# Another order of all work in a gated convolution block with a feed-forward: which queue issues ten of the loads, and when

## The chip, the core and the metric

The kernel runs on one NeuronCore of a Trainium2 chip. The metric is device time in microseconds (us), the median of three runs of the same kernel. The program's own profile gives, for one execution, when each instruction ran on each engine: PE (matrix products), DVE (elementwise), ACT (elementwise and eviction of results from PE's accumulators), POOL (GpSimd: here small statistics and DMA issues) and SP (here DMA issues alone).

## What is computed

With x = A_q of 2048 rows and 640 columns, the reference is, in short:

```python
k_shift = sum over t<4 of k[s - 3 + t] * shift_k[:, 3 - t]       # short causal convolution
kv = k_shift * v
y  = causal convolution of kv with ssm_k along 2048 rows (by FFT) + kv * ssm_D
h  = x + layernorm(x) * y
h2 = h + (silu(layernorm(h) @ w_gate) * (layernorm(h) @ w_up)) @ w_down    # F = 1728
```

All inputs and the output are bf16.

## The kernel before

The 2048 rows are four blocks of 512 (j = 0 to 3). For each block the kernel loads ssm_k (`load_g`), k (`load_k`), v and x, makes the spectrum G of ssm_k and the spectrum X of kv by matmuls with a fixed basis WF (`transform`, `forward`; line 329, evicted by ACT at line 319), multiplies and adds spectra of this block and of earlier ones on DVE (`window`, `mac`; lines 537 to 600), goes back with the basis WI (`inverse`, line 698), makes h and its row statistics, normalizes and transposes it (`turn_h`), and feeds it through the feed-forward layer (`ffn`): gate and up products (line 769), SiLU and product (lines 783 to 787), down product (lines 833 and 845). The feed-forward of block j stands among the convolution work of block j+1.

ssm_k must be transposed. Block 0's is transposed by PE (`transposed`, line 411). Blocks 1 to 3 are first regrouped by one ACT copy (`g_turned`, line 419) and then turned by four DMA transposes on SP (line 404); k of blocks 1 to 3 is turned by four DMA transposes each, straight from DRAM. kv is made by PE (the taps, line 490) and a DVE product with v (line 513). Nine matmuls of line 882 between two parts of block 0's taps feed nothing. ACT's sums for the row statistics of x and h are at lines 606 and 629; GpSimd finishes the statistics (lines 610 to 636).

All work is recorded as 923 operations with a number each; a recorded operation has a list of the buffers that it reads and writes. The tuple `ORDER` then says in which order they are handed out, and with that the order on each engine and queue, since every engine works through its own in turn. A negative number ~n hands out operation n in its other form: an eviction of ACT goes to DVE or back, a load goes to GpSimd's queue in place of SP's, and a sum of two buffers on DVE becomes an adding DMA from GpSimd:

```python
def load(nbytes, fn, w, r=()):
    return plan.add("sp", nbytes, lambda: fn(nc.sync), r, w, ("pq", nbytes, lambda: fn(nc.gpsimd)))
def added(ns, fn, to, what, reads, write, n=1):
    plan.add("dve", ns, fn, reads, [write], ("add", ..., lambda: nc.gpsimd.dma_start(out=to(), in_=what(), accum_op=ALU.add, ...)))
```

The order also decides the memory: large buffers lie in an arena of 22 units, and a buffer takes a unit when its first operation is handed out, so a load can have to wait until the last reader of the unit's buffer before is done. An accumulator `ps` has four places, a `row` five.

Of the kernel before, what the change touches and what calls it, by code (L numbers as in the profile page):

```python
# [47 lines left out]
    0, 1, 2, 3, 16, 18, -20, 5, 4, 8, 17, 186, 9, 20, 22, 7, 10, 11, -22, 24, -26, 23, 26, 75, 76, 13, 15, 12, 6,  # L48
    77, 78, 79, 193, 80, 81, 82, 34, 35, 14, 38, -40, 36, -38, 92, 32, 27, 93, 96, 97, 40, -42, 88, 89, 30, 94,
    95, 98, 99, 101, 102, 90, 91, 28, 84, 85, 42, 43, 44, 121, 119, 103, 29, 104, 118, 47, 48, 86, 87, 100, 45,  # L50
    46, 120, 105, 106, 49, 50, 124, 55, 51, 56, 83, 31, 52, 107, 108, 57, 58, 113, 33, 114, 53, 54, 123, 109, 110,
    67, 68, 125, 115, 126, 116, 111, 112, 194, 198, 192, 199, 117, 69, 70, 195, 59, 60, 71, 72, 196, 200, 201, 63,
    64, 61, 62, 73, 74, 127, 212, 65, 130, 66, 128, 202, 213, 207, 129, 134, 208, 131, 187, 203, 189, 197, 214,
    215, 216, 190, 209, 210, 204, 133, 205, 270, 188, 221, 224, 225, 223, 175, 132, 138, 122, 211, 206, 217, 143,
    144, 137, 136, 141, 222, 142, 140, 146, 218, 145, 147, 148, 226, 228, 227, 191, 229, 265, 178, 153, 154, 149,
    150, -165, -162, 135, 139, 151, 152, 235, 236, 245, 246, 237, 238, 162, 163, 220, 157, 219, 252, 247, 165,
    166, 248, 249, 231, 232, 409, 240, 155, 241, 156, 158, 159, 320, 325, 177, 336, 335, 180, 332, 173, 233, 253,
    242, 234, 239, 243, 244, 321, 174, 324, 328, 331, 271, 160, 250, 167, 310, 255, 334, 314, 338, 339, 168, 169,
    251, 337, 170, 176, 312, 333, 340, 341, 185, 416, 259, 323, 327, 171, 261, 172, 256, 326, 322, 329, 330, 269,
    -309, -255, 418, 267, 179, 309, 260, 311, 316, 347, 313, 315, 268, 317, 342, 262, 318, 230, 319, 353, 346,  # L60
    343, 350, 358, 357, 417, 266, 421, 422, 354, 381, 380, 385, 263, 257, 384, 383, 382, 345, 419, 349, 423, 348,
    386, 355, 424, -259, 264, 272, 273, 413, 344, 351, 352, 184, 361, 420, 360, 430, 431, 274, 275, 356, 359, 362,
    363, 375, 415, 432, 433, 435, 436, 376, 425, 437, 377, 438, 367, 370, 426, 277, 283, 378, 276, 279, 278, 290,
    427, 428, 410, 182, 181, 291, 282, 288, 289, 366, 434, 371, 414, 183, 281, 286, 287, 280, 284, 285, 295, 293,
    412, 296, 479, 294, 292, 439, 379, 297, 365, 369, 368, 411, 364, 372, 539, 483, 373, 374, 496, 503, 298, 299,
    429, 440, 387, 399, 300, 301, 389, 390, 391, 400, 401, 304, 392, 393, 402, 441, 442, 444, 448, 445, 305, 447,
    306, 307, 388, 302, 303, 394, 395, 396, 397, 404, 443, 475, 476, 477, 449, 451, 450, 446, 452, 498, 405, 406,
    478, 484, -482, 407, 408, 587, 588, 591, 454, 592, 455, 458, 459, 562, 485, -487, 590, 589, 593, 480, 456,
    457, 561, 565, 482, -617, 563, 398, 460, 461, 468, 469, 462, 463, 464, 564, 575, 566, 567, 470, 471, 465, 466,
    467, 472, 473, 453, 619, 576, 583, 502, 582, 584, -586, 586, 474, 490, 491, 579, 499, 541, 540, 544, 542, 620,  # L70
    543, 545, 546, 492, 493, 623, 624, 626, 618, 627, 569, 487, 577, 578, 549, 547, 580, 494, 581, 501, 489, 625,
    548, 551, 500, 497, 504, 403, 550, 552, 553, 488, 495, 505, 506, 507, 508, 509, 555, 568, 572, 554, 556, 558,
    557, 559, 560, 632, 633, 628, 640, 641, 636, 637, 634, 635, 642, 643, 638, 571, 513, 629, 630, 639, 519, 520,
    631, 510, 514, 521, 522, 570, 573, 574, 644, 526, 622, -646, 595, 611, 617, 511, 515, 516, 512, 517, 518, 687,
    525, 601, 612, 524, 527, 523, 528, 710, 682, 529, 530, 535, -534, 534, 531, 537, 532, 594, 596, 713, 646, 538,
    681, 602, 603, 606, 607, 707, 677, 685, 678, 680, 604, 608, 613, 614, 708, 597, 688, 609, 647, 649, 648, 651,
    598, 536, 806, 599, 805, 808, 650, 766, 765, 807, 809, 810, 811, 693, 709, 652, 654, 653, -622, 655, 695,
    -680, 768, 767, 711, 769, 770, 771, 683, 706, 800, 801, 802, -804, 690, 684, 665, 666, -687, -697, 712, 714,
    660, 758, -695, 661, 667, 668, 669, 759, 762, 662, 663, 670, 671, 689, 804, 761, 760, 656, 763, 691, -693,
    672, 673, 782, 657, 780, 764, 658, 674, 659, 664, 675, 676, 700, 702, 701, 787, 779, 788, 786, 790, 789, 791,  # L80
    792, 697, 783, 781, 784, 795, 773, 615, 785, 772, 775, 774, 776, 698, 777, 778, 699, -704, 704, 794, 793, 797,
    796, 798, 799, 812, 814, 815, 816, 705, 715, 716, 717, 718, 719, 600, 720, 605, 610, 817, 813, -758, 818, 819,
# [908 lines left out]
```

## Time and profile before

| | before |
|---|---|
| runs | 250.96, 251.34, 253.92 us; median 251.34 |
| the profiled execution | a span of 251.4 us from first to last instruction; the profile gives no other time of it |
| clock granted to PE | 1.000 |
| busy | PE 237.3 us, DVE 197.7, ACT 173.9, POOL 54.0 |
| DMA | 33.66 MB, 134 GB/s on the mean; SP's queue 21.38 MB, GpSimd's 11.96 MB |
| chain that ended last | PE 56%, ACT 17%, DMA 10%, DVE 9% |

"Idle before" in such a profile is time in which an engine had nothing running ahead of an instruction, and what ended it. "us to landing" of a DMA counts from its issue until the last byte is in. A window row gives the length, then busy time and instructions of PE, PE's weight loads, DVE, ACT and POOL, the clock, the share of the DMA engines' time that was busy, and GB/s.

### The profile page before, as it was taken

The page shows a single profiled execution, that of the slowest core. Times are in us where ns is not written, and L with a number is a line of the kernel's source. Part 1 is how long each engine was busy: PE and PEld are TensorE (multiplying, and loading weights), DVE is VectorE, ACT ScalarE, POOL GpSimd, SP SyncE. Part 2 cuts the span into 40 slices and gives each one's busy share as a digit, 9 for nine tenths or more (in the row PEclk, how much of TensorE's full clock was granted, in tenths as well). Part 3 has the DMA queues.
Part 4 walks back from the last instruction along what each step waited for, and adds up shares of the span by engine and source line. Part 5 has one row for each costly group of instructions (what it writes and reads, how often), then busy time and mean ns, then how long its engine had stood idle before and what let it go on. Part 6 is the DMA issues. An engine that isn't in the chain of part 4 may idle for free.

```text
span 251.4 us, 5138 instructions
## 1 busy us (share of the span) xinstructions
PE 237.3 (94%) x2113; PEld 153.0 (61%) x2125; DVE 197.7 (79%) x249; ACT 173.9 (69%) x300; POOL 54.0 (21%) x54
## 2 busy tenths in 40 slices
PE   3869997999999999999999999999999999999994
PEld 3447675788777677444465676454456785465662
DVE  2379999999999999999999989999999542131222
ACT  2449998999999976975988789983542865325100
POOL 0002003231540313220270404263612110000030
PEclk9999999999999999999999999999999999999999
DMA  5995699774998654685345468889592200000052
GB/s 156 376 212 163 127 324 352 231 197 92 165 246 292 202 81 81 105 154 133 79 66 146 86 99 194 148 146 163 98 224 29 26 0 3 0 0 3 0 78 78
DMA packets 37283, 33.66 MB, mean 134 GB/s; under 512 B 22470, under 2 KB 32076, under 8 KB 37260
## 3 DMA queue, kind: packets, MB, share of 16 engines
q1 hardware_dynamic: 31884, 21.38, 32.1%
q0 software_dynamic: 5376, 11.96, 25.9%
q8 instruction: 16, 0.26, 0.4%
q14 instruction: 7, 0.06, 0.1%
HBM read 16.29 MB, written 4.59 MB: 83 GB/s over the span
## 4 chain that ended last, share of the span: by engine, by line
PE 56%; ACT 17%; DMA 10%; DVE 9%; issue 4%; SPq 3%; DVEq 0%; ACTq 0%; POOLq 0%
PE ps L769 24%; PE ps L845 22%; ACT arena L319 7%; DMA arena<-in_A_ssm_k_dram 7%; PE ps L698 5%; DMA arena<-arena 3%; ACT sg L785 2%; PE ps L490 2%; SPq L404 2%; ACT junk L606 1%; PE ps L329 1%; PE ps L833 1%; DVE arena L674 1%; DVE arena L663 1%; DVE arena L662 1%
## 5 line engine op out<-in xcount | busy, mean ns | idle before, releaser
L769 PE MATMUL ps<-arena,wgu 128*128 128x512 bf16 (+1 forms) x668 | 116.7, 328 | 1.4 <-ACT sg L809 0.5
L769 PEld LDWEIGHTS <-wgu 128*128 128x128 bf16 x680 | 66.2, 98 | 45.3 <-issue 1.4
L845 PE MATMUL ps<-wd,tT 128*128 128x320 bf16 x416 | 59.1, 299 | 0.0
L845 PEld LDWEIGHTS <-tT 128*128 128x128 bf16 x416 | 39.8, 98 | 17.2 <-issue 1.8
L542 DVE TENSOR_TENSOR arena<-arena 128x2560 bf16<-128x2560 bf16 x30 | 44.1, 1484 | 0.2
L783 ACT ACTIVATE sg<-ps 128x1024 bf16<-128x1024 f32 (+1 forms) x28 | 26.9, 968 | 20.3 <-PE ps L769 19.7
L329 PE MATMUL ps<-arena,WF 128*128 128x320 bf16 x176 | 29.8, 299 | 1.2 <-ACT arena L319 0.9
L785 ACT CAST sg<-ps 128x1024 bf16<-128x1024 f32 (+1 forms) x23 | 23.0, 998 | 6.9 <-PE ps L769 3.1
L319 ACT CAST arena<-ps 128x320 bf16<-128x320 f32 (+1 forms) x48 | 25.2, 583 | 1.9 <-DVE arena L545 1.1
L610 POOL TENSOR_TENSOR sm<-sm,neghalf 128x4 f32<-128x4 f32 (+1 forms) x10 | 16.6, 1659 | 43.4 <-DVE sm L646 43.1
L787 DVE TENSOR_TENSOR tT<-sg,sg 128x1024 bf16<-128x1024 bf16 (+1 forms) x23 | 15.5, 673 | 11.5 <-ACT sg L785 11.5
L243 POOL DMA_DIRECT2D arena<-arena x11 | 13.3, 1211 | 47.4 <-DVE arena L542 11.2
L329 PEld LDWEIGHTS <-WF 128*128 128x128 bf16 x176 | 17.1, 98 | 10.0 <-issue 2.3
L606 ACT ACTIVATE junk<-arena 128x640 bf16<-128x640 bf16 x28 | 20.8, 744 | 1.3 <-DVE arena L709 1.3
L545 DVE TENSOR_TENSOR arena<-arena 128x2560 bf16<-128x2560 bf16 x14 | 20.7, 1487 | 0.2
L319 ACT ACTIVATE arena<-ps 128x640 bf16<-128x640 f32 (+1 forms) x32 | 20.2, 655 | 0.3
L698 PE MATMUL ps<-arena,WI 128*128 128x320 bf16 x96 | 15.7, 299 | 0.9 <-issue 0.6
L850 ACT ACTIVATE row<-ps,sm 128x640 bf16<-128x640 f32 x12 | 9.5, 791 | 8.2 <-PE ps L845 8.0
L709 DVE SCALAR_TENSOR_TENSOR arena<-arena,sm,ps 128x640 bf16<-128x640 bf16 x16 | 13.6, 876 | 1.8 <-ACT ps L707 1.8
L852 POOL DMA_DIRECT2D out_dram<-row x12 | 11.7, 1153 | 14.1 <-ACT row L850 14.1
L707 ACT ACTIVATE ps<-ps,sm 128x640 f32<-128x640 f32 x16 | 12.1, 770 | 3.7 <-PE ps L698 3.5
L698 PEld LDWEIGHTS <-WI 128*128 128x128 bf16 x96 | 9.0, 97 | 5.6 <-issue 1.3
(91 smaller groups left out, 240.8 us busy)
## 6 DMA issues: line engine op xcount, KB each, us to landing
arena<-arena POOLq DMA_DIRECT2D x11, 640.0 KB, 6.1
arena<-in_A_q_dram SPq DMA_DIRECT2D x4, 640.0 KB, 5.1
out_dram<-row POOLq DMA_DIRECT2D x13, 160.0 KB, 4.2
arena<-in_A_ssm_k_dram SPq DMA_DIRECT2D x3, 640.0 KB, 9.4
arena<-in_A_v_dram SPq DMA_DIRECT2D x3, 640.0 KB, 6.3
wd<-in_B_w_down_dram SPq DMA_DIRECT2D x2, 800.0 KB, 7.3
out_dram<-arena POOLq DMA_DIRECT2D x2, 640.0 KB, 5.8
wgu<-in_B_w_gate_dram SPq DMA_DIRECT2D x1, 800.0 KB, 6.5
```

Of the source, the lines that this page charges most:

```text
L319: (lambda: nc.scalar.activation(dst(), src(), ACT.Copy, scale=2.0)) if twice else (lambda: nc.scalar.copy(dst(), src())),
L329: nc.tensor.matmul(ap(ps)[:, h, 0:NH], w, ap(src)[:, r, h * NH:(h + 1) * NH], start=(first and i == 0), stop=(last and i == len(rs) - 1), ...
L542: dve(1402, lambda: v.tensor_mul(to(), X.part(xs), H.part(hs)), [X.at(xs), H.at(hs)], [at])
L545: added(1402 * n - 69 * (n - 1), lambda: v.tensor_add(to(), to(), b()), to, b, [what], at, n)
L606: act(725, lambda r=r: nc.scalar.activation(waste(), ap(x)[:, r, :], ACT.Square, scale=D ** -0.5, accum_out=sm(s, MSQ, (r,))), [(x, r)], [ ...
L610: nc.gpsimd.tensor_tensor(sm(s, RSTD, rs), sm(s, VAR, rs), ap(neghalf)[:, 0:len(rs)], op=ALU.pow)
L698: nc.tensor.matmul(ap(ps)[:, w, 0:NH], m, src[:, w * NH:(w + 1) * NH], start=(i == 0), stop=(i == len(terms) - 1))
L769: nc.tensor.matmul(split(ap(ps), n)[:, i, :], w(k), ap(hT)[:, k, lo:lo + n], start=(k == 0), stop=(k == KT - 1))
L783: act(905 if wide_ else 490, lambda: nc.scalar.activation(of(sg), of(*gate), ACT.Silu), [(gate[0], gate[1] + i) for i in range(m)] + (psu ...
L785: op = plan.add("act", 905 if wide_ else 490, lambda: nc.scalar.copy(of(co), of(*up)), psu + [sg], [co] + tt, ("dve", 1135 if wide_ else 6 ...
L787: op.rest = dve(602 if wide_ else 336, lambda: nc.vector.tensor_mul(to(), of(sg), of(co)), [sg, co], tt)
L845: nc.tensor.matmul(ap(ps[hf])[:, hf, 0:NH], ap(tT)[:, c * BLK + at:c * BLK + at + P], ap(wd)[:, c, hf * NH:(hf + 1) * NH], start=False, st ...
```

## The change

Only `ORDER` changes, in nearly every place, and the kernel loses one line by it, so line numbers after are smaller by one. The instructions are the same but for operations that take their other form: five more loads go out on GpSimd's queue (block 0's ssm_k, the first group of w_gate and of w_up, the last part of w_down, block 1's v) and two stores of the last block's output do, while block 3's v and another such store go back to SP; one more sum of spectra in block 3 is an adding DMA; a few evictions change between ACT and DVE.

```diff
 ORDER = (
-    0, 1, 2, 3, 16, 18, -20, 5, 4, 8, 17, 186, 9, 20, 22, 7, 10, 11, -22, 24, -26, 23, 26, 75, 76, 13, 15, 12, 6,
...
+    17, 8, 16, 26, 186, -13, 4, 5, 1, 0, 3, 7, 22, 24, -26, 13, 23, 9, 18, 10, 11, 20, 19, -22, 14, 75, 2, 6, 76,
...
```

SP's queue at the start of the program, before. The rows name the DMA's target and source; `arena` is whichever unit, `in_A_k_dram` k, `in_A_ssm_k_dram` ssm_k (first block 1's, then block 0's), `in_A_q_dram` x, WF and WI the bases.

```order
L477 DMA arena<-in_A_k_dram 128x1280
L889 DMA arena<-in_A_shift_k_dram 5x512
L477 DMA arena<-in_A_k_dram 128x1280
L289 DMA arena<-in_A_ssm_k_dram 128x5x512
L296 DMA arena<-in_A_v_dram 128x2560
L903 DMA WF<-const_wf 128x1024
L904 DMA arena<-in_A_ssm_D_dram 1x640
L289 DMA arena<-in_A_ssm_k_dram 128x5x512
L903 DMA WF<-const_wf 128x1024
L301 DMA arena<-in_A_q_dram 128x2560
```

SP's queue at the same place now:

```order
L476 DMA arena<-in_A_k_dram 128x1280
L888 DMA arena<-in_A_shift_k_dram 5x512
L476 DMA arena<-in_A_k_dram 128x1280
L295 DMA arena<-in_A_v_dram 128x2560
L288 DMA arena<-in_A_ssm_k_dram 128x5x512
L902 DMA WF<-const_wf 128x1024 x2
L903 DMA arena<-in_A_ssm_D_dram 1x640
L300 DMA arena<-in_A_q_dram 128x2560
```

v goes ahead of block 1's ssm_k, and block 0's is gone from this queue: it is GpSimd's first work now, ahead of the two instructions with which GpSimd's part began before. GpSimd's queue from the program's start through block 0, now:

```order
L288 DMA arena<-in_A_ssm_k_dram 128x5x512
L874 MEMSET neghalf 128x4
L871 ISA
L871 AFFINE_SELECT ident<-ident 128x128
L623 TENSOR_SCALAR sm_76<-sm_76 128x4
L609 TENSOR_TENSOR sm_76<-sm_76,neghalf 128x4
L295 DMA arena<-in_A_v_dram 128x2560
L609 TENSOR_TENSOR sm_78<-sm_78,neghalf 128x2
L736 DMA wgu<-in_B_w_up_dram 128x5x512
L753 DMA out_dram<-arena 128x2560
L736 DMA wgu<-in_B_w_gate_dram 128x5x512
L609 TENSOR_TENSOR sm_79<-sm_79,neghalf 128x2
```

The three loads in the middle and the store of h stood on SP before, or behind the last row shown.

SP's queue a little later, where block 1's x, the transposes of block 1 and the weights of the feed-forward go out, before:

```order
L404 DMA_TRANSPOSE arena<-arena 128x5x128
L301 DMA arena<-in_A_q_dram 128x2560
L404 DMA_TRANSPOSE arena<-arena 128x5x128 x2
L404 DMA_TRANSPOSE kT<-in_A_k_dram 128x5x128 x2
...
L737 DMA wgu<-in_B_w_gate_dram 128x5x640
L296 DMA arena<-in_A_v_dram 128x2560
L737 DMA wgu<-in_B_w_up_dram 128x5x576
L289 DMA arena<-in_A_ssm_k_dram 128x5x512
L737 DMA wgu<-in_B_w_gate_dram 128x5x576
```

and now:

```order
L403 DMA_TRANSPOSE arena<-arena 128x5x128 x2
L403 DMA_TRANSPOSE kT<-in_A_k_dram 128x5x128 x2
L300 DMA arena<-in_A_q_dram 128x2560
L736 DMA wgu<-in_B_w_gate_dram 128x5x640
L288 DMA arena<-in_A_ssm_k_dram 128x5x512
L736 DMA wgu<-in_B_w_gate_dram 128x5x576
L748 DMA wd<-in_B_w_down_dram 64x640
L736 DMA wgu<-in_B_w_up_dram 128x5x640
L736 DMA wgu<-in_B_w_up_dram 128x5x576
```

Block 1's x (the row with `in_A_q_dram`) went out behind the first transpose and now goes out behind all eight; block 2's ssm_k stands ahead of three of the weight loads, not of four, and its arena unit is now one that a sum of block 0's spectra still reads.

81 rows, old and new, of the table ORDER are left out of this document.

## The prediction

> **What bounds the kernel now.** I read the table of busy time and the slices first, then the waits, then stretches of the first 54 us, and last the order of time in the stretches that the change moves.
>
> ```profile
> core 0: 251.4 us, clock 1.000
> PE 237.3 (94%) x2113; PEld 153.0 (61%) x2125; DVE 197.7 (79%) x249; ACT 173.9 (69%) x300; POOL 54.0 (21%) x54
> PE   3869997999999999999999999999999999999994
> DVE  2379999999999999999999989999999542131222
> ```
>
> PE is busy for 237.3 of 251.4 us at full clock, which leaves 14.1 us of idle time. DVE is full as well from slice 4 to slice 27 (about 19 to 170 us), so the two run level for most of the program and a gain counts only if both get it. The change adds and removes no matmul. The most that it can win is therefore a part of those 14.1 us, and the first question is where they lie.
>
> ```profile
> PE ps L411 <- DMA arena<-in_A_k_dram: 4.0, 1, 4.0
> PE ps L411 <- DMA arena<-in_A_ssm_k_dram: 3.0, 1, 3.0
> DVE arena L513 <- DMA arena<-in_A_v_dram: 3.8, 1, 3.8
> DVE arena L413 <- PE ps L411: 3.5, 3, 1.6
> 36.00:42.00 6.00, 5.31 (x63) 3.36 (x61) 5.79 (x12) 5.07 (x12) 2.04 (x1) 1.00 1.07 357
> 42.00:48.00 6.00, 4.85 (x44) 3.89 (x44) 6.00 (x9) 6.00 (x12) 0.00 (x0) 1.00 1.05 338
> 247.98 0.55 DVE L864 SCALAR_TENSOR_TENSOR row<-ps,sm,arena 128x320 bf16<-128x320 f32 x1 [1.22 <-PE ps L845]
> ```
>
> Four us pass before the first half of k lands, 3.0 us go to the wait for block 0's ssm_k, 0.69 + 1.15 = 1.84 us are lost from 36 to 48 us (6.00 less 5.31 and less 4.85), and the tail behind the last matmul is 251.4 - 247.98 = 3.4 us. That is 12.2 of the 14.1. After 48 us PE hardly waits, so no later place has a gain of size to give; it can only lose.
>
> **The start, in order of time.** The wait of 3.0 us is the term on which the forecast rests.
>
> ```profile
> 1.65 0.36 SPq L477 DMA_DIRECT2D arena<-in_A_k_dram  x1
> DMA to landing us min/median/max: 3.1/3.1/3.2
> 2.05 0.43 SPq L289 DMA_DIRECT2D arena<-in_A_ssm_k_dram  x1
> 2.52 0.52 SPq L296 DMA_DIRECT2D arena<-in_A_v_dram  x1
> 3.90 0.38 SPq L289 DMA_DIRECT2D arena<-in_A_ssm_k_dram  x1
> 9.41 2.50 ACT L419 COPY arena<-arena 128x2560 bf16<-128x2560 bf16 x1 [2.57 <-DMA arena<-in_A_ssm_k_dram]
> 11.13 3.15 DVE L513 TENSOR_TENSOR arena<-ps,arena 128x512 bf16<-128x512 f32 x6 [3.83 <-DMA arena<-in_A_v_dram]
> 11.55 0.43 PE L490 MATMUL ps<-diag,kT 32*128 32x128 bf16 x28
> 14.96 1.03 PE L411 MATMUL ps<-ident,arena 128*128 128x128 bf16 x15 [2.98 <-DMA arena<-in_A_ssm_k_dram]
> 2.00:4.00 2.00, 0.00 (x1) 0.01 (x1) 0.00 (x0) 0.28 (x2) 0.00 (x0) 1.00 0.91 292
> 4.00:6.00 2.00, 2.00 (x20) 1.79 (x21) 1.19 (x6) 0.00 (x0) 0.00 (x0) 1.00 0.60 154
> 8.00:10.00 2.00, 2.00 (x71) 1.26 (x60) 0.00 (x0) 0.59 (x1) 0.00 (x0) 1.00 1.01 383
> 14.00:16.00 2.00, 1.04 (x17) 1.01 (x18) 0.53 (x2) 0.54 (x1) 0.00 (x0) 1.00 2.34 247
> ```
>
> The load at 1.65 is the second half of k, in at 4.8; the one at 2.05 is block 1's ssm_k, the one at 3.90 block 0's. PE has nothing to do between 11.55 + 0.43 = 11.98 and 14.96, when block 0's comes. Now GpSimd issues it as its first act, beside SP's first load. In bytes, k, v and both ssm_k are four times 0.655 MB, 2.62 MB. The stretches of before moved 0.58 MB by 4 us (292 GB/s), 0.31 MB from 4 to 6 and 0.77 MB from 8 to 10 (383 GB/s); from 4 to 6 us the DMA engines were only 0.60 busy, room that a second queue can fill. Even were that room left empty, 2.62 MB at 383 GB/s behind the 0.6 MB moved by 4 us end at 4 + 2.0 / 0.383 = 9.3 us; with the poor stretch it is near 10.5. Block 0's ssm_k is then there before 11.98, PE goes straight on, and the wait is gone: **-3.0 us**. What is late next is kv. Its six DVE products (3.15 us) waited for v at 11.13; v now stands ahead of block 1's ssm_k. Four of them can run while PE does its idle matmuls, the last two (a third of 3.15, 1.05 us) follow the taps at 11.98 and end near 13.0. PE has three transposes to do before the first forward matmul needs kv (x15, 1.03 us), also until 13.0, so kv costs nothing. DVE gains as much as PE: it starts the products some 2 us earlier, and most of the 1.47 us that it idles from 14 to 16 us (2.00 less 0.53) goes too.
>
> Costs at the start. (a) The new load shares the DMA engines with k, on which PE's first 4.0 us hang, at a share of 0.91. Nothing of before has both queues busy then. Lower end nothing; upper end 0.655 MB at 383 GB/s, 1.7 us, if it all went ahead of k. I look at when GpSimd's packets come: its one ssm_k load of before lands 5.7 us after issue.
>
> ```profile
> 111.68 0.93 POOL L289 DMA_DIRECT2D arena<-in_A_ssm_k_dram  x1 [5.06 <-DMA arena<-arena]
> DMA to landing us min/median/max: 5.7/5.7/5.7
> ```
>
> Of 5.7 us only 1.7 are moving at that rate, so most of its bytes should come 2 to 4 us after issue, when k (landing 3.1 us after issue) is nearly in. I take +0.4. (b) Block 1's ssm_k moves behind v; ACT's regroup of it (2.50 us) holds ACT until 11.9 before and, if v's 0.655 MB delay it fully, until 13.6. ACT's first eviction is due near 13.0. Between 0 and 0.6, I take +0.2. (c) Two copies of kT now stand first on ACT and the table that the Silu needs is loaded after them, a second ACT_TABLE_LOAD of 1.3 us; ACT then has nothing to do until the ssm_k lands (2.57 us idle in the row above), so nothing. (d) The identity that PE's transposes need is made after GpSimd's issue of 0.93 us, before k lands: nothing.
>
> **x and the weights.** Block 1's x, issued at 13.28 before, now stands behind all eight transposes on SP, since its slot was the regrouped ssm_k's.
>
> ```profile
> 22.21 2.53 SPq L404 DMA_TRANSPOSE kT<-in_A_k_dram  x2
> 32.08 0.82 ACT L606 ACTIVATE junk<-arena 128x640 bf16<-128x640 bf16 x1
> arena<-in_A_q_dram SPq DMA_DIRECT2D x4, 640.0 KB, 5.1
> DMA to landing us min/median/max: 7.5/7.5/7.5
> 18.00:24.00 6.00, 6.00 (x47) 4.33 (x45) 5.86 (x18) 6.00 (x19) 1.03 (x2) 1.00 0.62 182
> 24.00:30.00 6.00, 6.00 (x44) 4.08 (x43) 5.93 (x7) 6.00 (x16) 0.85 (x1) 1.00 0.63 126
> 32.41 0.82 DVE L594 TENSOR_TENSOR arena<-arena 128x1280 bf16<-128x1280 bf16 x1
> 28.74 0.58 SPq L737 DMA_DIRECT2D wgu<-in_B_w_gate_dram  x1
> 45.23 2.89 PE L769 MATMUL ps<-arena,wgu 128*128 128x256 bf16 x25 [0.16 <-ACT arena L413]
> ```
>
> The transposes start when the regroup ends, 11.9 to 13.0. Eight at 2.53 / 2 = 1.27 us are 10.2 us, the two WI issues among them 0.8 to 2.5 us; so x goes out between 22.9 and 25.7. At the median of 5.1 us it lands between 28.0 and 30.8, around 29.4. ACT squares it (L606) at 32.08 before, 2.4 earlier now, 29.7. I take no cost; the upper end, with the landing time of the load that went out at 13.28 (7.5 us, 33.2), is 3.5 us.
>
> The weights for block 0's first gate and up chunks follow on SP, with block 2's ssm_k among them, whose slot is free only when the DVE sum at 32.41 is done: 33.2 - 2.4 = 30.8. Behind it on SP are three weight loads (0.74, 0.82 and 0.74 MB) and a small one, with it 3.0 MB. At the 338 to 357 GB/s of the stretches 36 to 48 us they are in by 30.8 + 3.0 / 0.338 = 39.7, some 41 with the latency. PE's first L769 stood at 45.23, now 42.8, and reaches the last of these matrices four chunks later: no wait. The two remaining weights go out on GpSimd behind the first L610, and are used last.
>
> **The rest of the program.** GpSimd's added issues (0.93 us each) go out ahead of row statistics that wait for DVE anyway. The added adding transfer, the last of block 3, takes a DVE sum of 1.48 us away; that DVE time goes to evictions which it now does for ACT. The transfer goes out when the product of L542 at 180.12 is done, lands a median 6.1 us later, and is needed by the sum of L582; in the new order DVE has four operations of 1.48 and two of 0.68 us between the two, 7.3 us, and an eviction besides.
>
> ```profile
> arena<-arena POOLq DMA_DIRECT2D x11, 640.0 KB, 6.1
> 180.12 1.48 DVE L542 TENSOR_TENSOR arena<-arena 128x2560 bf16<-128x2560 bf16 x1
> 187.54 1.48 DVE L582 TENSOR_TENSOR arena<-arena 128x2560 bf16<-128x2560 bf16 x1
> ```
>
> For hundreds of small swaps elsewhere I take nothing: they can win at most the 1.84 us of 36 to 48, and lose up to the landing of one add. The tail keeps its last matmuls, sum and SP stores.
>
> **Sum.** -3.0 + 0.4 + 0.2 = -2.4 us on a span of 251.4, so **249.0**. The median of the runs is 251.34, level with the span, so nothing is added for what lies around it.
>
> **Rivals.**
> 1. k is delayed. If the load of (a) and k take equal turns, the second half of k is in when twice k's bytes have moved, 1.31 MB, at 4 + 0.7 / 0.383 = 5.8 us and not 4.8: 1.0 in place of 0.4, 249.6. If GpSimd's goes ahead of k altogether, 1.7 in place of 0.4, 250.3. For it: the share of 0.91 from 2 to 4 us. Against it: the latency of GpSimd's load. The Trainium skill, "DMA: Bandwidth & Descriptors", section "Queues, rings and completion order", says that each DMA engine goes round the queues for which it has work, packet by packet; by that rule the equal turns are the likelier of the two, and no run here shows both queues loading at that moment.
> 2. x is late, the way to a slower kernel. ACT works in order, and behind L606 stand kv's evictions and the inverse's, for which PE and DVE both wait. With x landing at 33.2 ACT stalls 3.5 us: 252.5. It decides from a landing of 32.1 on, where the stall has eaten the 2.4 us. For it: eight transposes ahead on one queue. Against it: DMA engines 0.62 to 0.63 busy from 18 to 30 us, not the full load in which 7.5 us was measured.
> 3. The change doesn't do what it says: GpSimd's first load lands no earlier than 14.9, or WF, which is behind both ssm_k, takes the place of the wait. WF's 0.52 MB at 383 GB/s end 1.4 us behind the rest, near 12; a wait of 1 to 3 us gives 250 to 251.4.
> 4. A later wait: one adding transfer that is needed 2 to 5 us before it lands, in a stretch where DVE has no slack: 251 to 254, and beyond 256.4 if it happens more than once.
> 5. The small swaps win: the 1.84 us go and (a) and (b) cost nothing: 251.4 - 3.0 - 1.84 = 246.6.
>
> **How the numbers follow.** Forecast (248.2 to 249.4) 0.45, first rival 0.13, second 0.12, third 0.08, fourth 0.12, fifth 0.10. About 2% is what a measurement of this kernel can tell from no change, 246.3 and 256.4. The range 246.8 to 252.8 leaves out the fifth rival and the upper part of the fourth, and has the upper end of x in it. Faster than 246.3 needs the fifth rival and a little more: 0.07. Slower than 256.4 needs more than one wait of the fourth: 0.06. The rest, 0.87, is within 2%.
>
> **What would show it.** PE's L411 behind the taps starts near 12.4, not 14.96, with no wait for ssm_k over 0.5 us; ACT's first L605 near 29.7 with no idle time ahead of it; from there on PE's and DVE's events stand 2 to 3 us earlier than before, to the end. I am wrong if k's first landing moves past 5 us, if ACT or PE names x, a weight or an adding transfer in its waits with more than 1 us, or if the first 30 us gain 3 us and the end doesn't.

## The result, and the profile after

The changed kernel takes 253.73 us (median of 20 runs, 252.26 to 259.09), the kernel before on the same chip 251.58 (20 runs, 250.43 to 254.52): a ratio of 1.0075, 95% interval 1.0053 to 1.0097. The forecast of 249.0 with a range of 246.8 to 252.8 missed, and in the wrong direction: 0.75% slower where 1% faster was expected. A ratio, here and below, leaves out executions that ran in a slower state, so it is not the quotient of the two medians beside it.

The profiled execution of the changed kernel spans 251.8 us, that of before 251.4. Time and span are not the same: in every execution whose span is on record the time is 1.65 to 1.78 us longer. So the profiled execution of the changed kernel took 253.45 us, near its median, while the 251.4 of before stand for about 253.1 us (an estimate, with the same difference), longer than 16 of its 20 runs. A comparison of these two profiles therefore shows less of a loss than the runs do.

The changed kernel's busy times, and then PE's waits (us in total, times, the longest):

```profile
PE 238.2 (95%) x2125; PEld 153.0 (61%) x2125; DVE 197.2 (78%) x250; ACT 172.9 (69%) x298; POOL 60.7 (24%) x60
```

```profile
PE ps L410 <- DMA arena<-in_A_k_dram: 5.2, 2, 3.8
PE ps L768 <- DMA wgu<-in_B_w_up_dram: 1.2, 1, 1.2
PE ps L328 <- ACT arena L412: 0.9, 1, 0.9
PE ps L328 <- DVE arena L514: 0.7, 1, 0.7
```

The wait for block 0's ssm_k (3.0 us) is gone, as forecast. In its place stand 1.2 us more of k (two waits of 5.2 us in all, where one of 4.0 stood), 1.2 us for w_up, 0.9 for an eviction by ACT (L412) and 0.7 for a product on DVE (L514, kv of block 1). What follows is the order of time of PE, ACT and DVE:

```profile
6.67 1.25 PE L410 MATMUL ps<-ident,arena 128*128 128x128 bf16 x10 [1.36 <-DMA arena<-in_A_k_dram]
8.16 2.12 PE L489 MATMUL ps<-diag,kT 32*128 32x128 bf16 x112 [0.25 <-ACT kT L412]
12.75 0.43 PE L489 MATMUL ps<-diag,kT 32*128 32x128 bf16 x28
13.11 1.06 PE L410 MATMUL ps<-ident,arena 128*128 128x128 bf16 x15
14.46 0.44 PE L410 MATMUL ps<-ident,arena 128*128 128x128 bf16 x5
15.76 1.44 PE L328 MATMUL ps<-arena,WF 128*128 128x320 bf16 x9 [0.86 <-ACT arena L412]
30.41 0.70 PE L697 MATMUL ps<-arena,WI 128*128 128x320 bf16 x4 [0.15 <-ACT arena L318]
12.54 2.59 ACT L418 COPY arena<-arena 128x2560 bf16<-128x2560 bf16 x1 [2.91 <-DMA arena<-in_A_ssm_k_dram]
32.29 0.74 ACT L605 ACTIVATE junk<-arena 128x640 bf16<-128x640 bf16 x1 [0.74 <-DMA arena<-in_A_q_dram]
10.73 3.28 DVE L512 TENSOR_TENSOR arena<-ps,arena 128x512 bf16<-128x512 f32 x6 [2.29 <-DMA arena<-in_A_v_dram]
```

The loads, each with the time from issue to landing: the second half of k (issued at 1.66), v (2.06), block 1's ssm_k (2.53) and block 0's on GpSimd (1.35):

```profile
DMA to landing us min/median/max: 5.0/5.0/5.0
DMA to landing us min/median/max: 8.5/8.5/8.5
DMA to landing us min/median/max: 9.9/9.9/9.9
DMA to landing us min/median/max: 9.0/9.0/9.0
```

For the comparison, two rows of PE's order of time in the kernel before:

```profile
6.58 2.44 PE L490 MATMUL ps<-diag,kT 32*128 32x128 bf16 x112
31.13 0.70 PE L698 MATMUL ps<-arena,WI 128*128 128x320 bf16 x4 [0.15 <-ACT arena L319]
```

Read it downwards. The second half of k lands at 1.66 + 5.0 = 6.7 us, not 4.8, and PE's taps start at 8.16, not 6.58: 1.58 us lost. PE reaches the first transposes of block 0's ssm_k at 13.11 where it stood waiting until 14.96: 1.85 gained, since the wait of 2.98 us is gone and the taps with the nine idle matmuls take 0.4 us less (12.75 - 8.16, against 11.55 - 6.58). Then ACT comes: its regroup of block 1's ssm_k starts at 12.54 and holds it until 15.13, and PE waits 0.86 us for ACT's eviction (L412) that stands behind. At the group of the inverse's matmuls that has a wait of 0.15 us for ACT in every run (**the marker** from here on, at 31.13 before) only 31.13 - 30.41 = 0.72 us is left. The expectations below count it from its first weight load, 0.45 us earlier ("PE at 30 us").

The second half of the story is the stretches from 36 to 48 us, where PE has 0.93 and 1.80 us of idle time, against 0.69 and 1.15 before, and its wait of 1.2 us for the last part of w_up, which was in at 39.5 us before (8.1 us after its issue at 31.38). The stretches, then PE's row with that wait and the last DVE instruction:

```profile
36.00:42.00 6.00, 5.07 (x60) 3.23 (x58) 5.96 (x11) 5.92 (x14) 2.56 (x2) 1.00 1.03 306
42.00:48.00 6.00, 4.20 (x36) 2.81 (x34) 6.00 (x11) 6.00 (x12) 1.79 (x3) 1.00 1.07 357
```

```profile
48.30 5.96 PE L768 MATMUL ps<-arena,wgu 128*128 128x256 bf16 x53 [1.18 <-DMA wgu<-in_B_w_up_dram]
248.49 0.55 DVE L863 SCALAR_TENSOR_TENSOR row<-ps,sm,arena 128x320 bf16<-128x320 f32 x1 [1.22 <-PE ps L844]
```

The last DVE instruction stands at 248.49, 0.51 us behind before's 247.98. So by the profiles the gain at the start shrank to 0.7 us, and between 36 and 50 us it turned into a loss of 0.5. No adding transfer and no x appears among PE's waits.

But x reaches PE by a detour. ACT idles 0.74 us for x before L605 (above), so its scaling of the inverse's results (L706) comes later, DVE idles 0.94 us for that, and the product on DVE that gives PE block 1's kv (L514) comes later in turn. DVE's rows after and before, then PE's row and its first gate product, both after (45.23 before):

```profile
35.99 0.88 DVE L708 SCALAR_TENSOR_TENSOR arena<-arena,sm,ps 128x640 bf16<-128x640 bf16 x1 [0.94 <-ACT ps L706]
35.83 0.88 DVE L709 SCALAR_TENSOR_TENSOR arena<-arena,sm,ps 128x640 bf16<-128x640 bf16 x1
40.80 1.23 PE L328 MATMUL ps<-arena,WF 128*128 128x320 bf16 x6 [0.73 <-DVE arena L514]
45.05 1.80 PE L768 MATMUL ps<-arena,wgu 128*128 128x256 bf16 x15 [0.19 <-ACT arena L412]
```

Of the 0.72 us at the marker 0.18 are left at 45 us, before the wait for w_up begins.

### The profile page after: what moved, and what is told of

Read it like the earlier page. It is cut to its first block, busy times and chain, and to the rows that moved or that the text cites. A ratio compares the mean times of both kernels' runs of the same rounds, so it can differ in the third digit from the quotient of the medians.

```text
span 251.8 us, 5166 instructions
## 1 busy us (share of the span) xinstructions
PE 238.2 (95%) x2125; PEld 153.0 (61%) x2125; DVE 197.2 (78%) x250; ACT 172.9 (69%) x298; POOL 60.7 (24%) x60
## 4 chain that ended last, share of the span: by engine, by line
PE 72%; DVE 11%; DMA 6%; issue 4%; POOL 2%; ACT 2%; SPq 1%; DVEq 0%; POOLq 0%; ACTq 0%
PE ps L768 35%; PE ps L844 23%; PE ps L328 7%; DMA arena<-arena 3%; PE ps L489 2%; DMA arena<-in_A_k_dram 2%; DVE arena L708 2%; POOL sm L609 2%; DMA arena<-in_A_q_dram 2%; PE ps L697 2%; DVE arena L541 2%; PE ps L832 1%; PE ps L881 1%; PE ps L410 1%; DVE tT L786 1%
## 5 line engine op out<-in xcount | busy, mean ns | idle before, releaser
L844 PE MATMUL ps<-wd,tT 128*128 128x320 bf16 x416 | 59.7, 299 | 0.0
L844 PEld LDWEIGHTS <-tT 128*128 128x128 bf16 x416 | 39.7, 98 | 17.2 <-issue 2.1
L541 DVE TENSOR_TENSOR arena<-arena 128x2560 bf16<-128x2560 bf16 x30 | 43.8, 1485 | 0.1
L609 POOL TENSOR_TENSOR sm<-sm,neghalf 128x4 f32<-128x4 f32 (+1 forms) x10 | 17.7, 1770 | 47.3 <-DVE sm L645 47.0
L318 ACT CAST arena<-ps 128x640 bf16<-128x640 f32 (+1 forms) x47 | 24.7, 586 | 4.3 <-PE ps L328 4.1
L242 POOL DMA_DIRECT2D arena<-arena x12 | 14.6, 1220 | 48.8 <-ACT ps L706 18.5
L784 ACT CAST sg<-ps 128x1024 bf16<-128x1024 f32 (+1 forms) x22 | 21.1, 957 | 7.0 <-PE ps L768 5.8
L786 DVE TENSOR_TENSOR tT<-sg,sg 128x1024 bf16<-128x1024 bf16 (+1 forms) x22 | 14.3, 650 | 13.1 <-ACT sg L784 13.1
L605 ACT ACTIVATE junk<-arena 128x640 bf16<-128x640 bf16 x28 | 20.6, 738 | 1.2 <-DMA arena<-in_A_q_dram 0.7
L318 ACT ACTIVATE arena<-ps 128x640 bf16<-128x640 f32 (+1 forms) x32 | 19.4, 649 | 1.5 <-PE ps L328 1.3
L544 DVE TENSOR_TENSOR arena<-arena 128x2560 bf16<-128x2560 bf16 x13 | 19.2, 1485 | 0.1
L708 DVE SCALAR_TENSOR_TENSOR arena<-arena,sm,ps 128x640 bf16<-128x640 bf16 x16 | 13.6, 876 | 2.3 <-ACT ps L706 2.3
L706 ACT ACTIVATE ps<-ps,sm 128x640 f32<-128x640 f32 x16 | 12.0, 778 | 2.1 <-PE ps L697 2.1
```

Source lines behind the costliest of these rows:

```text
L318: (lambda: nc.scalar.activation(dst(), src(), ACT.Copy, scale=2.0)) if twice else (lambda: nc.scalar.copy(dst(), src())),
L541: dve(1402, lambda: v.tensor_mul(to(), X.part(xs), H.part(hs)), [X.at(xs), H.at(hs)], [at])
L544: added(1402 * n - 69 * (n - 1), lambda: v.tensor_add(to(), to(), b()), to, b, [what], at, n)
L605: act(725, lambda r=r: nc.scalar.activation(waste(), ap(x)[:, r, :], ACT.Square, scale=D ** -0.5, accum_out=sm(s, MSQ, (r,))), [(x, r)], [ ...
L609: nc.gpsimd.tensor_tensor(sm(s, RSTD, rs), sm(s, VAR, rs), ap(neghalf)[:, 0:len(rs)], op=ALU.pow)
L708: dve(800, lambda r=r, ps=ps, s=s: v.scalar_tensor_tensor(two(ap(x)[:, r, :]), two(ap(x)[:, r, :]), sm(n1, MEAN, (r,)), half(ap(ps)), op0= ...
```

## The experiments

Theories: in the first four runs **A** (the start gains 0.7 us, the weights lose it, more goes later), **B** (the start loses) and **C** (all of the loss is late); then, for what ate the gain at the start, **K** (the second half of k, delayed by GpSimd's load) and **R** (ACT's late regroup), and for the weights **W**, **Q** and **N**, as the expectations define them. In the kernels from the fifth on every buffer keeps the place that it had in the kernel that is edited, so that only the order moves. Line numbers shift by some 46 by the table that does this. A time stands beside that of the kernel before on the same chip.

| run | edit | us (range, runs) | before | ratio, interval | span | marker |
|---|---|---|---|---|---|---|
| e1 | new start, old rest | 252.3 (251.6 to 253.7, 12) | 252.5 | 0.999 (0.996 to 1.003) | 251.9 | 30.53 |
| e2 | old start, new rest | 260.3 (258.8 to 262.9, 6) | 252.5 | 1.029 (1.023 to 1.035) | 257.6 | 31.19 |
| e3 | new to 62 us, old rest | 259.1 (256.8 to 265.9, 6) | 252.5 | 1.021 (1.014 to 1.028) | 255.1 | 30.83 |
| e4 | the changed kernel | 253.1 (252.1 to 256.5, 12) | 252.5 | 1.000 (0.997 to 1.004) | 250.7 | 30.39 |
| e5 | changed, ssm_k of block 0 third on SP | 253.7 (252.8 to 258.3, 12) | 252.0 | 1.007 (1.003 to 1.010) | 251.1 | 31.37 |
| e6 | changed, no regroup of block 1 | 256.9 (255.7 to 259.6, 6) | 252.0 | 1.017 (1.010 to 1.024) | 255.8 | 29.31 |
| e7 | before, ssm_k of block 0 on GpSimd | 253.0 (252.1 to 254.6, 12) | 252.0 | 1.005 (1.002 to 1.009) | 252.3 | 30.77 |
| e8 | before, ssm_k of block 0 ahead of WF | 251.8 (250.5 to 253.5, 12) | 252.0 | 0.998 (0.994 to 1.002) | 249.5 | 29.11 |
| e9 | before | 252.3 (251.3 to 257.2, 12) | 251.8 | 0.999 (0.995 to 1.003) | 251.0 | 29.65 |
| e10 | changed, first loads on SP | 256.1 (254.7 to 257.2, 6) | 251.8 | 1.014 (1.008 to 1.020) | 255.5 | 30.58 |
| e11 | changed, last part of w_up early | 253.4 (252.0 to 254.2, 12) | 251.8 | 1.004 (1.000 to 1.007) | 251.6 | 30.20 |
| e12 | both of these | 251.7 (250.8 to 252.0, 12) | 251.8 | 0.998 (0.996 to 1.001) | 249.7 | 29.38 |
| e13 | changed, weights off GpSimd | 253.4 (252.3 to 254.8, 12) | 252.4 | 1.005 (1.001 to 1.009) | 250.7 | 30.49 |
| e14 | e10, weights off GpSimd | 253.1 (250.7 to 254.8, 12) | 252.4 | 1.000 (0.996 to 1.005) | 251.1 | 29.32 |
| e15 | the changed kernel | 253.7 (251.4 to 259.4, 12) | 252.4 | 1.003 (0.998 to 1.008) | 251.0 | 30.73 |
| e16 | e12 again | 251.5 (250.7 to 253.1, 12) | 252.4 | 0.997 (0.994 to 1.000) | 249.0 | 29.14 |
| e17 | before | 252.2 (251.1 to 254.4, 12) | 252.5 | 0.999 (0.995 to 1.002) | 251.2 | 31.14 |
| e18 | e8 again | 251.8 (250.9 to 253.9, 12) | 252.5 | 0.996 (0.992 to 1.000) | 249.4 | 29.48 |

**Halves of the two orders (e1 to e3), and the changed kernel again (e4).** Each takes the first operations from one order and all others, as they follow, from the other:

```diff
 ORDER = (          # e1; e2 and e3 likewise, with 215 numbers of before and 345 of the change
-    0, 1, 2, 3, 16, 18, -20, 5, 4, 8, 17, 186, ...
+    17, 8, 16, 26, 186, -13, 4, 5, 1, 0, 3, 7, ...    # 200 numbers of the change, then the rest of before's
```

> The first 200 operations as now (to about 33 us), the rest in the order of before. Theory A (the traces of before and after, read as they stand): the start still gains, but only 0.7 us at 30 us, since k's second half lands 1.9 us later and eats most of the 3.0; so 250.9, 0.997 of before, k in at 6.6 and PE's inverse products 0.7 us ahead. Theory B (the profiled execution of after was a kind one, and in most executions k lands later still): 252.5 or more, 1.004 and up. Theory C (all of the loss sits late): 0.997 or below.

> The first 215 operations as before (to about 33 us), the rest in the new order. Theory A (the start gains 0.7 us, the weights of block 0 lose 1.2 us, and 1 to 2 us more go in the late part): 254.2, 1.010 of before, with a wait of PE for w_gate or w_up between 42 and 50 us. Theory B (the start loses): 251.6 to 252, 1.000 to 1.002. Theory C (late part alone): 1.007 to 1.010, no wait for weights.

> The first 345 operations as now (to about 62 us), the rest in the order of before. Theory A: the wait for the weights is in, the late part is not: 251.58 - 0.7 + 1.2 = 252.1, 1.002. Theory B (start and weights hold the whole loss): 253.5, 1.007. Theory C (late part alone): 250.9 to 251.6, 0.997 to 1.000.

> The changed kernel once more, for a second profile and a ratio on the same chip as the three above: 1.0075 within its interval (1.005 to 1.010). Theory A: k's second half in at 6.6 us again, PE waiting 1 to 3 us for weights, about 0.5 us behind before from 60 us to the end, and the rest of the difference in the late part. Theory B: k's landing differs from one execution to the next by 1 us or more and PE is late from the start. Theory C: level with before until 100 us.

e1 is as theory A has it in the trace (marker 30.53, 0.60 ahead of before's first profile), but the time is level with before. e2 and e3 are failed experiments: they lose 6 to 8 us, in waits that neither kernel that they are made of has in this size. In e2 PE waits for weights between 36 and 56 us, shortly behind the seam of the two orders at 33 us; in e3 for an eviction at 102 us, 40 us behind its seam at 62. That operations of one order meet buffers that the other still holds is a likely cause, and not shown. PE's waits in e2 from 36 to 56 us, then PE's row in e3:

```profile
PE ps L767 <- DMA wgu<-in_B_w_gate_dram: 1.9, 1, 1.9
PE ps L767 <- DMA wgu<-in_B_w_up_dram: 1.5, 1, 1.5
```

```profile
105.39 0.43 PE L327 MATMUL ps<-arena,WF 128*128 128x320 bf16 x2 [3.64 <-ACT arena L317]
```

So they say nothing on theory C. e4 does: in the second profile of the changed kernel the wait for w_up isn't there at all and the span is 250.7, 0.7 us below before's. From the marker to the last DVE instruction the changed kernel takes 218.08 us in its first profile, which has the wait of 1.2 us for w_up, and 217.00 in the second; before takes 216.85. These profiles have no sign of a late loss, which speaks against theory C; as e4's profiled execution (252.35 us) was shorter than its median (253.13), a late loss in longer executions is not excluded.

**The start, one suspect at a time (e5 to e8).** The edits, as they stand in the order (12 is block 0's ssm_k on SP, -13 the same on GpSimd, 26 v, 186 block 1's ssm_k, 13 and 14 WF; e6 leaves the ACT copy out and lets the transposes read its source):

```diff
-    17, 8, 16, 26, 186, -13, 4, 5,           # changed kernel
+    17, 8, 16, 12, 26, 186, 4, 5,            # e5
-    -20, 5, 4, 8, ... 75, 76, 13, 15, 12, 6, # before
+    -20, 5, -13, 4, 8, ... 75, 76, 13, 15, 6,  # e7
+    -20, 5, 4, 8, ... 75, 76, 12, 13, 15, 6,   # e8
-            act(2414, lambda: nc.scalar.copy(...
+            act(2414, None if j == 1 else lambda: nc.scalar.copy(...    # e6
```

> The changed kernel, with block 0's ssm_k back on SP as third large load (behind both halves of k, ahead of v); all else and every buffer's place as now. Theory K (the second half of k, 1.9 us late because GpSimd's load shares the DMA engines with it, is what ate the gain): k in at 4.8, PE's taps at 6.6 and not 8.2, PE at 30 us 1.3 to 1.6 us ahead of the changed kernel. Theory R (ACT's regroup of block 1's ssm_k, which now ends at 15.1 us and not at 11.9, binds): PE reaches the first transposes near 12.0 and then waits for ACT until 15; at 30 us 0 to 0.4 ahead of the changed kernel.

> The changed kernel without ACT's regroup of block 1's ssm_k: the DMA transposes read it as it was loaded, so block 1's spectrum of ssm_k isn't the reference's. Theory R: PE's waits between 14.2 and 15.9 us (0.84 and 0.30 us) go, and PE stands 1.0 us ahead of the changed kernel from 18 us on. Theory K: the waits go to another evictor (DVE), 0 to 0.3 us.

> The kernel before with one move: block 0's ssm_k goes out on GpSimd as its first act. Block 1's ssm_k stays ahead of v. Theory K: k's second half lands at 6.2 to 6.9 and not 4.8, PE's taps start 1.6 us later, the wait for ssm_k (3.0 us) is gone, and v, in near 12.5 and not 11.0, delays kv: at 30 us 0 to 1.0 ahead of before, 250.6 to 251.6. Theory R: with the regroup done before 13.5, the whole of 3.0 less 0.4 to 1.0 stays: 2.0 to 2.6 ahead, 249.2.

> The kernel before with one move: block 0's ssm_k on SP ahead of both halves of WF and not between them. Both theories: k in at 4.8, block 1's ssm_k at 9.4, v at 11.0 as before, block 0's ssm_k at 12.7 and not 14.9, the first half of WF near 13.3 where PE needs it at 13.7; PE's wait falls from 3.0 to 0.7 us, PE 2.2 us ahead of before at 30 us. If the gain at the start is kept to the end, 249.4 (0.991); if later waits for weights or DVE swallow it, 251 to 251.6 (0.998 to 1.000) with new waits between 36 and 70 us.

e5 brings k's second half back (in at 4.7) and PE's taps to 6.80, and yet its marker stands at 31.37, not ahead of the changed kernel's 30.41 but behind it. The order of time of PE, and of ACT's regroup, in e5 shows why:

```profile
6.80 2.13 PE L535 MATMUL ps<-diag,kT 32*128 32x128 bf16 x112 [0.25 <-ACT kT L458]
12.39 0.44 PE L456 MATMUL ps<-ident,arena 128*128 128x128 bf16 x5 [0.23 <-DVE arena L558]
13.59 0.77 PE L456 MATMUL ps<-ident,arena 128*128 128x128 bf16 x10 [0.76 <-DVE arena L558]
14.74 0.45 PE L374 MATMUL ps<-arena,WF 128*128 128x320 bf16 x2 [0.38 <-DMA WF<-const_wf]
16.09 1.18 PE L374 MATMUL ps<-arena,WF 128*128 128x320 bf16 x7 [0.63 <-ACT arena L458]
12.88 2.57 ACT L464 COPY arena<-arena 128x2560 bf16<-128x2560 bf16 x1 [4.62 <-PE ps L456]
```

PE arrives 0.7 us earlier (12.39, not 13.11), and waits in turn for DVE (kv's products, which need v), WF and ACT (behind the regroup, here until 12.88 + 2.57 = 15.45; its row names PE, but block 1's ssm_k lands only at 3.11 + 9.7 = 12.8). Theory K alone is refuted: k's delay is real, but taking it away gains nothing while v, WF and the regroup are late. e6 takes the regroup away, and PE waits for ACT no more after the transposes. Its marker is 1.1 us ahead of the changed kernel's 30.41 and 30.39:

```profile
29.31 0.70 PE L743 MATMUL ps<-arena,WI 128*128 128x320 bf16 x4 [0.15 <-ACT arena L364]
```

Theory R is the better one, with a caution: this is one execution, and k's second half came at 5.9 in it, which is 0.3 to 0.7 us of the gain. (e6's time is no verdict on the start; it has a wait of 5.2 us for w_up, below.) e7 puts GpSimd's load into the old order, where the regroup is early and v is late instead: the marker gains 0.36 us, the time loses 0.5%. (Its profile has a wait of PE of 1.7 us at 152 us for a DMA transpose, which no other profile has; whether that is the loss is not shown.) Each order pays somewhere: k, v, both ssm_k and WF are wanted by 13 us, and an early landing of one is a late landing of another. e8 shows the way out: with block 0's ssm_k ahead of WF only, PE waits 1.3 us and not 3.0, and 2.0 us are gained at the marker. They last to the end, as e8's order of time shows for PE and DVE:

```profile
12.41 0.47 PE L457 MATMUL ps<-ident,arena 128*128 128x128 bf16 x5 [1.31 <-DMA arena<-in_A_ssm_k_dram]
29.11 0.70 PE L744 MATMUL ps<-arena,WI 128*128 128x320 bf16 x4 [0.15 <-ACT arena L365]
246.01 0.55 DVE L910 SCALAR_TENSOR_TENSOR row<-ps,sm,arena 128x320 bf16<-128x320 f32 x1 [1.21 <-PE ps L891]
```

The last DVE instruction is 1.97 us ahead of before's first profile. The timed runs show less, 0.998: the median span on that chip is 250.0 for e8 and 250.25 for before, so the 1.97 us compare a short execution of e8 with a long one of before.

**How far one profile can be trusted (e9, e17), and e8 again (e18).** Kernels unchanged.

> The kernel before, unchanged, for a second profile. Theory P (the span of one profiled execution scatters by 1 us, and that of before was a long one): 250.0 to 250.7, PE at 30 us at 30.0 to 30.7. Theory S (spans repeat to 0.3 us, and the timed executions of the changed kernel lose something that its profiles don't show): 251.1 to 251.7. Ratio 1.000 within 0.004 by both.

> The kernel before a third time. Theory V (the wait for block 0's ssm_k, 3.0 us in the profile that the prediction was read from and 1.0 us in the second, is a draw of each execution): block 0's ssm_k in between 13.3 and 15.0 us, PE's first transposes of it between 13.4 and 15.1, PE at 30 us between 29.1 and 30.8. If 3.0 us is the rule and the second profile the exception: 14.9 and 30.7 again. If 1.0 us is the rule: 13.4 and 29.2.

> The kernel before with block 0's ssm_k ahead of both halves of WF on SP, a second time. PE at 30 us again at 28.7 within 0.3. If the wait of before is 3.0 us as a rule, its time is 0.992 of before; if it is 1.0 as a rule, 0.997 to 0.998, as in its first measure (0.998).

Block 0's ssm_k takes from its issue at 3.9 us to landing, in the first, the second and the third profile of before:

```profile
DMA to landing us min/median/max: 11.0/11.0/11.0
...
DMA to landing us min/median/max: 9.5/9.5/9.5
...
DMA to landing us min/median/max: 11.0/11.0/11.0
```

PE's first transposes of it and the marker in the second profile, and the transposes in the third:

```profile
13.48 1.03 PE L411 MATMUL ps<-ident,arena 128*128 128x128 bf16 x15 [0.85 <-DVE arena L513]
29.65 0.70 PE L698 MATMUL ps<-arena,WI 128*128 128x320 bf16 x4 [0.15 <-ACT arena L319]
```

```profile
14.97 1.03 PE L411 MATMUL ps<-ident,arena 128*128 128x128 bf16 x15 [2.96 <-DMA arena<-in_A_ssm_k_dram]
```

Theory V holds: in the second profile the load was in 1.5 us earlier, the wait had become 0.85 us for a DVE product, and the marker stood at 29.65, ahead of every profile of the changed kernel (30.41, 30.39, 30.73). In e2, whose start is before's, it is 3.2 us again: the long wait is the more frequent, three of four, but not the rule. Over three profiles each the marker is at 30.64 before and at 30.51 after, a gain of 0.13 us. The span of e9 is 251.0 all the same, for PE loses 1.6 us at 37 us (0.6 in the first profile), in an idle time that the profile puts down to "issue". The three profiled spans of before agree to 0.4 us, as theory S has it, but all its executions together do not: in the five batches timed with e1 to e18 its spans run from 249.1 to 254.6 us, with medians of 250.1 to 250.8. So theory P has the right reason, though e9's own span lies above its 250.0 to 250.7, and S is refuted in its second half too: no execution loses anything between span and time beyond the 1.65 to 1.78 us that all have. The three profiles of before fell on executions longer than its median. e18 repeats e8: 29.48 and 0.996.

**The weights (e10 to e16).** 178 is the last part of w_up; -175 and -174 are the first group of w_up and of w_gate on GpSimd, 174 and 173 the same on SP:

```diff
-    17, 8, 16, 26, 186, -13, 4, 5,
+    17, 8, 16, 186, 26, 12, 4, 5,            # e10, e12, e14, e16: first loads on SP
-    -192, 175, 228, ... 155, 178, 338,
+    -192, 175, 178, 228, ... 155, 338,                # e11, e12, e16
-    177, -175, 185, ... 334, 184, 339, ... 255, -174, 309,
+    177, 185, ... 334, 184, 174, 173, 339, ... 255, 309,    # e13, e14
```

> The changed kernel, with the first loads put as in the run before with the single move: block 1's ssm_k, v and block 0's ssm_k in this order behind k on SP, none of them on GpSimd. Theory KR (k's delay and the late regroup, together, cost the start 1.3 us): k's second half in at 4.8, the regroup done at 11.9, PE at 30 us at 28.7 and not 29.95. Then the profiled span is 249.4 to 250.5, and the time 1.2 us below the changed kernel's. If something else holds PE back between 14 and 30 us: 29.5 or later.

> The changed kernel, with one load moved: the last part of w_up (0.74 MB), which PE waited for at 46.6 us, goes out behind the last part's first w_gate load and not as the sixth. Theory W (in the timed executions this wait is usual, and costs 1 to 2 us): no wait for w_up between 45 and 50 us, 252.0, 0.996 of the changed kernel. Rival (the wait passes to the next load, w_gate or the other w_up, which are pushed back by 0.74 MB at 338 GB/s, 2.2 us): a wait of 1 us or more for another part of wgu, and no gain.

> Both edits, the first loads and the last part of w_up, on the changed kernel. Theories KR and W: 250.5 to 251.3, 0.994 to 0.998 of before, a profiled span near 249.5. If the start alone counts: as the run with the first loads alone. If neither: 253, 1.005.

> The changed kernel, with the first group of w_gate and w_up back on SP, behind the other weights, and no longer on GpSimd. Theory Q (GpSimd's two loads of 0.66 MB go out at 41 to 43 us on a queue of their own and take half of the DMA engines' time from the last part of w_up, which is still waiting on SP): SP has the engines nearly to itself from 38 to 46 us, the last part of w_up is in before 46 us, no wait at 46.6 us, and the time falls by 1 us or more against the changed kernel on the same chip. Rival N (the load is late by its place as sixth on SP, whatever GpSimd does): wait of 0 to 1.5 us as now, time unchanged, or a new wait near 53 us for the group that was moved.

> The same with the first loads on SP too (block 1's ssm_k, v, block 0's ssm_k in this order), as in the run whose profile has a wait of 4.8 us for w_up. Theory Q: that wait goes, 251.7, 0.998 of before, and 4 us below that run. Rival N: a wait of 3 to 5 us stays, 255 to 256.

> The changed kernel a third time, beside the two above. If the wait for w_up differs from one execution to the next (1.2 and 0 us in its two profiles so far), the time stays 1 to 2 us above before on this chip and its timed executions spread over 3 us or more. PE at 30 us again at 29.9 within 0.3.

> The changed kernel with the first loads on SP and the last part of w_up early, a second time: 0.998 of before within 0.003, timed executions within 1.5 us of each other, since neither the start nor w_up has a wait that scatters. Rival: 0.993 or below, if its first measure fell on a poor chip.

e10 is a miss that taught most. Its marker (30.58) gains nothing, because block 0's ssm_k landed at 14.4 in that execution; and PE then stands still for 4.8 us. PE's row, two stretches, and the time from issue to landing of the last part of w_up:

```profile
51.40 2.95 PE L814 MATMUL ps<-arena,wgu 128*128 128x256 bf16 x13 [4.79 <-DMA wgu<-in_B_w_up_dram]
```

```profile
48.00:50.00 2.00, 0.00 (x0) 0.00 (x0) 2.00 (x5) 2.00 (x3) 0.01 (x1) 1.00 0.98 381
52.00:54.00 2.00, 2.00 (x12) 1.43 (x10) 2.00 (x1) 0.00 (x0) 2.00 (x1) 0.50 0.80 155
```

```profile
DMA to landing us min/median/max: 14.7/14.7/14.7
```

It needs 14.7 us from its issue at 36.7 (8.1 us before the change), while the DMA engines are full (0.98, 381 GB/s). e12 differs from e10 in the place of that one load: the wait is 0.2 us, the time 251.7 and not 256.1. e14 leaves it where it is and takes GpSimd's two weight loads away instead: 0.4 us, 253.1. So each of the two cures the wait when the first loads are on SP, which speaks for theory Q as far as the wait goes; the place of the load counts as much. In the changed kernel itself, whose waits are 1.2, 0 and 0 us in three profiles, neither cure moves the median (e11 253.4, e13 253.4, e15 253.7), as rival N has it: theory W in the form that the usual execution pays 1 to 2 us for weights is refuted. e15 came as expected, 1.3 us above before and spread over 8 us. The first loads do move it where w_up is early: e12 stands 1.7 us below e11, and e16 2.1 us below e15 (there both edits count). With the other cure they bring 0.3 by the medians (e14 against e13) and 0.5% by the ratios, in executions that spread from 250.7 to 254.8. The marker agrees: with the first loads on SP it stands at 29.38, 29.32 and 29.14 (e12, e14, e16), where the regroup is done by 11.7 us and k's second half is in by 5.5, and at 30.20 to 30.83 in the seven profiles with the changed kernel's first loads and its regroup (its own three, e1, e3, e11, e13). e10 is the exception. The marker and the end of e16, the best version:

```profile
29.14 0.70 PE L743 MATMUL ps<-arena,WI 128*128 128x320 bf16 x4 [0.15 <-ACT arena L364]
245.82 0.55 DVE L909 SCALAR_TENSOR_TENSOR row<-ps,sm,arena 128x320 bf16<-128x320 f32 x1 [1.22 <-PE ps L890]
```

It doesn't clearly beat before: 0.998 and 0.997, with intervals that reach to 1.001 and 1.000. e8, one move on the kernel before, does as well: 0.998 and 0.996, the second with an interval from 0.992 to just under 1.000.

## Why the prediction was wrong

**The wait of 3.0 us as a gain: mis-sized.** It went, as said. But it was read from one execution. A second one of the same kernel has 0.85 us in its place, so that the most that could be won on average was less. The point that the prediction made of its 3.0, that PE would go straight on at 12.4, came to 13.11, 13.56 and 13.16 in the three profiles.

**(a) k delayed, +0.4: mis-sized.** The second half of k landed at 6.7, 6.2 and 6.4 us, against 4.8, 5.8 and 5.5 before: 1.9 by the first profiles, beyond the upper end of 1.7, and 1.1 on the mean. The argument that GpSimd's bytes come late, taken from a load at 111 us, failed. The rule of the Trainium skill, "DMA: Bandwidth & Descriptors", section "Queues, rings and completion order", that each DMA engine goes round the queues packet by packet, was the better guide: rival 1, which by equal turns has 1.0 in place of 0.4, is near the mean of 1.1. GpSimd's load didn't go ahead of k altogether: it needed 9.0 us.

**(b) Block 1's ssm_k behind v, +0.2: the step that failed by a wrong count.** I let v's bytes alone go ahead of it and had the regroup end by 13.6 at most. But block 0's ssm_k goes ahead of it too, on the other queue: twice 0.655 MB at 383 GB/s are 3.4 us behind the 9.4 of before, 12.8. Measured 12.4, and ACT was held until 15.13. e6 without the regroup gains 1.1 us at the marker, 0.4 to 0.8 of it not to be put down to k, e5 with k restored nothing. The sum of bytes that had all four loads in by 10.5 let the loads behind them wait (WF ends "1.4 us behind the rest" in the third rival). By 12.4 us, when block 1's ssm_k was in, the stretches of the changed kernel add up to about 3.4 MB, some 0.7 MB more than the four loads (an estimate from their GB/s): loads issued later on the same queue, WF and x, had moved bytes by then, and the first half of WF was in 0.7 us later, at 13.1.

Sum at the start: 2.4 forecast, 0.72 by the first profiles, 0.13 on the mean of three. kv, which I had cost nothing, is part of it: in e5 and e7 PE waits for DVE's products, which wait for v.

**x, 0: mis-sized.** x went out at 27.70 and not by 25.7, since the transposes wait for the late regroup, and landed at 32.2; ACT's first L605 stood at 32.29, not 29.7, and ACT idled 0.74, 0.23 and 0.31 us for it in the three profiles. In the first this took 0.73 us of PE's time at 40 us by the order of time above, through ACT and DVE as the second rival has it, though not its 3.5 us; no run moves x alone. In the other two PE waits 0.45 and 0.46 us for the same product of DVE, which had no idle time for ACT there and was late by itself; before has no such wait in any of its three. ACT's second table load cost nothing, as said.

**Weights, 0: failed.** The prediction had all of them in by 41 us, from SP's bytes alone. GpSimd's loads of v and of the first group and its store of h share the engines, four times 0.655 MB: 2.62 / 0.338 = 7.8 us on top of 39.7 are 47.5 (an estimate), and the last part of w_up, sixth on SP, came at 48.3 in the first profile. PE waited 1.2, 0 and 0 us for it in the changed kernel, 4.8 and 5.2 in its variants e10 and e6. That PE reaches it "four chunks later" was wrong as well: PE asks for it at 47.1, right behind the matmuls at 46.69 and 2.1 us behind its first gate product.

**The rest, 0, and the adding transfer: right.** No wait for an adding transfer appears in any profile of the changed kernel. From the marker to the end it loses 1.23 us against before's first profile with the wait for w_up, and 0.15 and 0.20 in the two profiles without.

**The base, a span read as a time: a term put at nothing.** The prediction found the median of 251.34 level with the span of 251.4 and added nothing for what lies around the span. That is 1.7 us in every execution whose span is on record; the two were level because the profiled execution was a long one. So its 249.0 is a span, and as a time 250.7. With what the first profiles show, 1.7 us less gain at the start (0.72 for 2.4) and 1.2 us lost behind the marker, 249.0 + 1.7 + 1.7 + 1.2 = 253.6, beside the 253.73 measured.

**What stays open.** The three profiles put the changed kernel level with before (spans of 251.8, 250.7 and 251.0 against 251.4, 251.0 and 251.2), while its timed runs are 0.75, 0.02 and 0.28% slower, a spread wider than the intervals of two of them. The spans of all executions explain the difference: the profiles of before lie above its medians, those of the changed kernel below its own (252.0, 251.4 and 252.0). What a longer execution of the changed kernel loses, and where, no profile shows. That the order of the first loads costs the changed kernel time is shown by e12 against e11, one edit apart and timed together: 1.7 us, of which the marker shows 0.8. With w_up early this is as much as the kernel loses against before (e11 1.6 us above it, e12 level); that it is the whole of the changed kernel's loss is not shown. Nor is why the last part of w_up takes 14.7 us in e10 and at most 13.3 in the changed kernel (issued behind 35.0, its wait over at 48.3), with the same loads around it.

## What to carry to other kernels

A wait for a load at the program's start, when five loads share the DMA engines, is no gain to be booked at its length: count all loads that will now stand ahead of each, on every queue, and ask which consumer becomes the last. Take a second profile of the same kernel before resting a forecast of 1% on one wait, and see first how the profiled execution's time compares with the median of the runs: a wait that only a long execution has is not there to be won in the others. A load that is moved back by bytes on one queue is moved back again by what the other queues send at that time.

## What the runs showed of the hardware

- The same load, issued at 3.9 us in the same kernel, was in after 11.0, 9.5 and 11.0 us. Others vary so too: the first half of WF was in at 13.1, 14.8 and 13.2 us in the three profiles of the changed kernel, the second half of k at 6.7, 6.2 and 6.4.
- GpSimd's load, issued at 1.35 us, ahead of all but the first of SP's large loads, landed at 10.4, 10.6 and 10.4 us, level with SP's v of the same size issued at 2.06 (10.6, 10.6 and 10.7).
- After PE's wait of 4.8 us in e10 the granted clock was 0.50 from 52 to 54 us and 1.00 until 50; the wait of 3.0 us at 12 us leaves it at 1.00. The Trainium skill, "TensorE: Matmul & The Clock Gate", section "What's actually happening", gives half rate after an idle window of about 3.4 us, with which both agree. e3's wait of 3.64 us left the clock at 1.00 too (from 104 to 108 us). Two us at half clock are about 1 us of PE's work (an estimate), so a wait that grows from 3 to 5 us can cost more than its length.
